# A new hand-out order for the matrix products of an attention-and-MLP kernel, and a later place for one small product

## The chip, the cores and the metric

The kernel runs on one core of a Trainium2 chip. The metric is the device time of one execution, in microseconds (us): the median of three runs. A core has a matrix engine (TensorE, PE in the profile), three engines for elementwise work (VectorE, DVE; ScalarE, ACT; GpSimd, POOL), and SyncE (SP), which here only issues transfers. Products are accumulated in eight PSUM banks; a bank holds 128 partitions by 512 float32 values. All other tiles lie in the on-chip memory SBUF, and DMA queues, which the engines issue to, bring data from and to the chip's DRAM.

## The reference

Two stages: an attention block over four batches of 12,480 tokens of 128 features, then a two-layer perceptron over all 49,920 tokens.

```python
# x[4,12480,128], inducing[32,128]; scale = 1/sqrt(128)
def mab(q, kv):
    a = softmax(scale * (q @ kv.T))
    return a @ kv
h = mab(inducing, x)        # 32 rows of 128 for each batch
y = mab(x, h)               # every token: weights over the 32 rows of h
# w_in[128,2048], w_out[2048,128], alpha[2048]
t = y @ w_in
g = maximum(t, 0) + alpha * minimum(t, 0)
out = g @ w_out             # float32, [49920,128]
```

## The kernel before

**How the work is folded.** A token's `y` is a mix of the 32 rows of `h`, so `y @ w_in` is the token's 32 unnormalised weights times `hW = h @ w_in`. The first layer is thus a product over only 32 rows. The exponentials of the scores are made batch by batch (`e`, written to DRAM as `e2d`, and read back as the tile `rep`, in which the 32 weights of the tokens stand in the 32 partitions of each of the four row tiles). Normalisation is left to the end: the finished output is multiplied by the reciprocal of the sum of weights (`rdT`).

The activation is split in two. Its relu part goes through `W1 = (1 - alpha) * w_out`. The rest is linear in `t`, so it needs no wide layer: `Amat = w_in * diag(alpha) * w_out` (128 by 128) is made once, and `hA = h @ Amat` once per batch. `Amat` takes 16 products of `winT` and `AW` (alpha times `w_out`, made on POOL) that are added up in one bank; this is `w_amat` (lines 952 to 959), called `am` in the tables, and `hA` is made by `h_linear` (line 632), called `hl`.

**Groups, fills and second products.** The tokens are worked on in 100 groups, 25 per batch: 24 of 512 tokens and one of 192. TensorE's 128 rows are used as four row tiles of 32 rows, numbered 0 to 3, on which products of 32 rows can run side by side. A group has 16 *fills* (`fill`, line 733), 4 per row tile: a 32-row product of `hW` and `rep` writes 128 channels by 512 tokens into a bank, and ScalarE (line 750) or VectorE (line 752) evicts the bank with a relu into a bf16 tile `gt`, of which there are 80. (The group of 192 tokens has 8 fills of two products each.) After that come the *second products* (`second`, line 784): each `gt` tile is multiplied with `W1`, again in four parts of 32 rows, and all 64 parts of a group are added up in one bank, the group's *home*. Row tile 0 does its 16 parts of a group, then row tile 1, and so on; on one bank a row tile starts only when the one before it is through (`hand_over`). The product with `hA` is one more product into the same bank. The last three groups (`WHOLE = 3`) use products of all 128 rows instead, 16 for each group. When row 3 has ended a group, `finish` (line 809) transposes the bank on VectorE (line 818), multiplies it with `rdT` on POOL (line 826), and POOL issues the transfer to the output (line 851).

**The order.** Nothing is scheduled by a program: every engine's order is written out by hand. The string `PLAN` is read token by token (the loop at the end of the function), and `pin` holds every engine to the order in which instructions are issued:

- `a` to `h`, with a digit for the bank: a fill. The letter's index divided by two is the row tile; even letters (a, c, e, g) are evicted by ScalarE, odd ones (b, d, f, h) by VectorE.
- `w`, `x`, `y`, `z`: the next second product of row tile 0, 1, 2, 3.
- `l` and `m`, with a digit for the bank: a group gets its home bank. For groups from the third on (`LATE = 2`) the product with `hA` is issued here; for the first two it is issued at the group's end. `v` is a whole product of 128 rows, for the last three groups.
- `s`, with digits for banks: a pause. The functions of the next line of `PAUSES` are called, with those banks to work in, and then those of the line with the same key in `BEHIND`.
- a lone digit 0 to 3: a *useless* product (`useless`, line 761) on that row tile. It multiplies old `xT` data into bank 4 + r, and nobody reads it.

`PAUSES`, `EVENTS` and `BEHIND` are keyed by group and fill. `EVENTS` are run just before the fill with that key. A pause, however, stands where its `s` stands in `PLAN`; its key only sets the order of the pauses. Before the change `am` is issued ahead of fill 32 (counting all fills from 0) and `hl0` ahead of fill 42.

The functions behind the names that matter here: `rep` loads a `rep` tile from `e2d`, four transfers on SP's queue; `new` takes new tiles for a batch; `xa` transposes the first half of a block of `x` for the next batch, by transposing transfers on SP's queue; `den` makes the sums of weights, whose reciprocal comes back as `rdT` over SP's queue.

Of the kernel before, what the change touches and what calls it, by code (L numbers as in the profile page):

```python
# [30 lines left out]
1 8 am  # L31
2 2 hl0
# [35 lines left out]
1 8 rep01  # L68
# [120 lines left out]
1 8 new1 xa10  # L189
# [14 lines left out]
3zwc4wzwf1zxwe6zwh7xwzc3wzxwg4d1wzxwe6xzwf7zwzc3ywywzd4ywzc1yzl6yxwg7yxg3wxywh4xywxya1xywxyh2a7x  # L204
ywxyb3xya4xywd1ywxe2wxzf7s342zf1xwzxwe3zxwf7zwc2zwyc4zwyd1zwyzyc3zyxb7zyxg2yxb4zyxza1yxzyxb3ze7x
zyxl2yxwg4yxwyxwg1yxwh3yxwxg7wf4xzwxe0zwze1wzywd3zywzyc7wzyd4wzyc0wzwf1zwyza3yza7xyzb4xyza0xzyxl
1zyxwyxwg3yxwh7xywg4yxwh0xywg5xwzxe3wxzwf7xzwxze4wxf5zwc0zwzd3yws745d0wzywyzc3b7yzyzxa4yzxl5yzxb
0yzxa3yzxwzxywxg7ywxg4ywyxh0wyg3xwyxwyxh7wxe6wxzf4wxze0wxze3wzwd7zywc6zywzywd4zyc0zyxb3zyxzya7xz
yb6xzya4xzyl0xzywxg3ywxzywxg7ywxyh6wxywg4xe3wxzwxf2zwxzwe7xzwe4d6zwyzwyd3zwyzc2wyzd7wyza6yzl4xyz
wxyg3b2xyzxwyza6xyzb7xyzwxyg3wxyg2wxyh6ywxwxwxe7zs312xzb7e6xzwf3xzwe2xzwzwc1zywd6yzwc7yzwd2yzwza  # L210
3yzyb1xyzxa6zyxl7zyxwh2yxa3yxzwyxwg6yxwg1yxwyxwh3yxwg2xwe6xwzf5xwzxwze1xwzf3c2wzwzywd6yzwc5yzyzd
# [12 lines left out]
yg2wxyg5wxyh4wxwxf1zwxe3zwzwc2yzwyd5wzyc4wzyzl3d1yzwxyza2xyzwxf5zwxe4zwxyzb1xyza2xywzxyzwc5ywxyg
4wxyg1b2xywxywxe5b7xzwe4xzwd2zwxe1zwd5zwyc7zwyzc4yb2zxyl1zxywzxya5h7yxwzyxwg4d2ywzywxza5yxzyb7xz
xywg4ywxzywxg2yxwe5wxf7wzxf4xzws2657wxzf2wzc4wzyd6wzyc7l5zywwzxywwwzxe2b4zxywwzxywa7h6xywwxzywwx
zwe2wb4xyzwxwzya7xzyl6xywxg2ywxyh4wxywg7xywxwf0c2zwyxzxwxyxh4wc7yzxwyxzxwxe2d0zwyxzxwyxzwc7f4zxw
yxzxwyc2zb0yxzxxyza7xyzb4xyzxya2zxyzl0xywg7xywxyh4ywyxe2zwxyzwyxyyh3we7xzwyxyzywyxe4h2wxyzwyxyyz
wyc7f3zwyzwyc4zwyd2zwyzwc7yzyb3zxya4zxyzxa2yzxl7yzxzwyzzxa3zf4zxzwzyzxzwzyg2xywh1xwyzxg3wyxzzwxz
ze4wzxf2wzxwe1zxwzf3c5wzywzyc4wzyd2wzyc1zwyb3zyza5xyzxyb4zxya2zxyl1xzywxze3xwyh5xwyg4xwyxwyg2xwy  # L230
h3s6452xzwf3xzwe6xzwe4xzwf2xzwc5zwzwyd3wzywd6zywc4zya2zyl5zyxwh3yxwzyxwg4yxb6zyxwzyxa2yzxwyxwyg3
xwyxh4ya6xwe2xwxzf0wxzwxe3zwxzf6wzc4wzywd2zywc0zyzya3zxb6yzxyl4zxywzc2b0yzxywzxya3zxywg6xywxyh2w
xywg0xyg3wxywh7xwe6xzwxzwf2xzwe0xzwd3zwyzc7wyzwyza6d2yzl0xyzwxyg3wd7yzwxyzwxe6zb2xyzwxyza3xyzwxy
a7xywh6xyg2wxywxyg3wxf1wxwzxe7wzxf2zwc6zwyzwd3yzc1yzxa7yzxb2yzxl6yzxwyzc3b1yzxwyzxwyg7xb2yzxwyzx
we3zwxyg1wxywxywxh7ys23517xwzf2xwze3xwzf7c5wzwzyc1wzyd2wzya3zyzyxb7zyxa5zyxb1zyxl2zyxwze3xwzyd7w
yxg5wyxzwyxg1wyxg3wyxh7wyxwxg5wxzf1wxze4wxzwzd3wzyc7wzyd5wzyc1l4zyxwzyxa3zf7xwzyxwze1xzb5yxzwyxz
a3yxzwyxg7wyxwh1yxa5yxwg3yxwyxh0wyxwe7xwzf5wc1zywzywd3zywc0zya7zyxb5zyxl1zyxwzyc3b0zyxwzyxwg7f5x
wzyxwzyxa3zf0xwzyxwg7yxwzyxwg5yxwf3xwe0zxwzxwze7wd6zywzywc5yzd0l3zwxe7zwxzyb6xzywc5yzwxyzxb0yzxa
7zyxwyh6xa5yzxwyzxwyg0xwyxwg7yxwyh5xws60275h6we0xwzxwzd2e5zyc7wzywzyd0l6zyxwzyxa5zyd2wzyxwg7yxwz
f0xwzyxa5zyxwh2yxwze7xwzyxwh0yxa5yzxwyxza2yxg7wxwzxf0wze5wzywd2zywc4zya7zyxzb0yxzl5yxzwyxg2b4yxz  # L240
wyxzwyc7h0wyxzwyxza2yxh4wyxzwyc7zwyxzwe0xwf2zxwzxe4wzxwzxe7wzd0wzywzc1yl4zd2ywzxya7zxywh0xywzc1y
wzyxb2zyxa7zyxwzyxa0zyxwg1yxwyxwh2yxwg7yxwxf0we3xzwf1xzwze2xwzwzc7wyzd0yl3zwyxzya2xh1ywxzxya7zxy
b0zxywzc2wyzd1wyzxa7yzwxyzwxyg0wxyh2xwyg1wxye7wxwxzf0s6127f0zxwe6zxwzd1we7zwyzc2yzxyb0zxyzxya6zy
xb7zyxa1zyxl2zyd0wzyxwg6yxwh7yxwzyc1wzyxwg0yxwh6xywxwe7xzwxe1zwxzwf0c5zwyzwd7yzwc6yzwd1yza0yzxl5
yzxwyzxa7f6zxwyzxwyg0xb1yzxwyzxa7yzxwyg6xwyh0xwyxg1wyxwe7xwzxf4wzxe6wzwzyd1wzyc0wzyd7wzya4zya6xz
yxzb1yxzl0yxzwyd7zwe4xzwyxzwe6xzwyxg1wyxwh4yxwyg7xwyxh6wyxa3xe1wzxwzf4xwze7wzywzd3ywzc6yl1zyxwh4
yxwg7yxwzyxb3zyc6wzyxwzyxa4h7yxwzyxwzyd3a6zyxwzyxwg4yxwzxe7wzxwzxb6s34273e6wzd4f7wzxe2wzxs3yc6wz
# [876 lines left out]
```

## Time and profile before

| | us |
|---|---|
| three runs | 541.54, 541.55, 541.62 |
| median | 541.55 |
| the profiled execution: its span | 540.4 |
| TensorE busy | 526.3 (97%) |
| VectorE busy | 504.2 (93%) |
| ScalarE busy | 496.3 (92%) |
| GpSimd busy | 394.7 (73%) |

The profile is of one execution. Its span, from the first to the last thing recorded, is 540.4 us; the runs' times hold about 1.15 us more, which lie outside of the span. "Busy" is the time in which an engine worked on at least one instruction. For TensorE this says little here, since four row tiles can work at once and one is enough to count as busy. Other views used below: the groups of instructions (line, engine, operation, output tile `<-` input tiles, shape, count, then busy time, mean in ns, and idle time ahead of them with what ended it), the chain of waits (start, length, engine, what), the timeline (start, length, engine, line, what), and stretches of the span (start:end, length, then busy time and instruction count of PE, PEld, DVE, ACT, POOL, the granted share of TensorE's clock, the busy share of the DMA engines, and GB/s).

### The profile page before, as it was taken

The numbers are of one execution on the slowest core, as the hardware profiler recorded it, in microseconds if no ns is written. First come the engines' busy times: TensorE is split into PE (matmuls) and PEld (weight loads), VectorE is DVE, ScalarE is ACT, GpSimd is POOL, SyncE is SP. The second block draws the span as 40 slices with busy tenths as digits, with TensorE's granted clock in tenths as the row PEclk, the third lists the DMA queues.
The fourth block names the chain that finished last, engine by engine and source line by source line (L and its number), as shares of the span: only waits on it lengthen the run. The fifth ranks groups of instructions, "written<-read, shape, count | busy, mean of one in ns | idle before, by whom it ended". The sixth has DMA issues, their size and how long they took to land.

```text
span 540.4 us, 21603 instructions
## 1 busy us (share of the span) xinstructions
PE 526.3 (97%) x8988; PEld 332.7 (62%) x8988; DVE 504.2 (93%) x865; ACT 496.3 (92%) x994; POOL 394.7 (73%) x574
## 2 busy tenths in 40 slices
PE   4999999999999999999999999999999999999996
PEld 4655566566567566666667666666666566666653
DVE  3699999999989999999998999999999999999994
ACT  2499999999989999999999999999999999999950
POOL 5553778687667987687687987776767876776764
PEclk9999999999999999999999999999999999999998
DMA  8999999987799898887799797864354344334324
GB/s 197 212 186 139 182 185 156 170 142 113 112 175 149 134 160 152 162 129 145 117 153 166 117 164 158 168 101 113 66 93 113 66 96 112 70 89 108 68 42 85
DMA packets 114738, 71.12 MB, mean 132 GB/s; under 512 B 86784, under 2 KB 102784, under 8 KB 114640
## 3 DMA queue, kind: packets, MB, share of 16 engines
q0 software_dynamic: 19456, 38.62, 38.9%
q1 hardware_dynamic: 91984, 30.22, 32.9%
q8 instruction: 70, 1.15, 0.9%
q10 hardware_dynamic: 3200, 0.90, 0.7%
q14 instruction: 28, 0.23, 0.2%
HBM read 41.00 MB, written 28.95 MB: 129 GB/s over the span
## 4 chain that ended last, share of the span: by engine, by line
PE 90%; DMA 4%; DVE 2%; ACT 1%; POOL 1%; issue 1%; SPq 0%; POOLq 0%; DVEq 0%
PE bank L383 90%; DMA xn<-in_x_dram 2%; DMA rep<-e2d 1%; ACT gt L750 1%; DVE gt L752 1%; DMA e2d<-e 1%; POOL xn L412 0%; DVE ot L818 0%; PE bank L458 0%; ACT e L656 0%; DVE xT L461 0%; POOL ob L826 0%; DVE fr L608 0%; SPq L671 0%; POOL out_dram L851 0%
## 5 line engine op out<-in xcount | busy, mean ns | idle before, releaser
L383 PE MATMUL bank<-gt,W 32*128 32x512 bf16 (+1 forms) x6256 | 480.3, 371 | 0.1
L750 ACT ACTIVATE gt<-bank 128x512 bf16<-128x512 f32 (+1 forms) x906 | 464.5, 612 | 6.9 <-PE bank L383 4.6
L752 DVE TENSOR_SCALAR gt<-bank 128x512 bf16<-128x512 f32 (+1 forms) x662 | 417.7, 677 | 9.9 <-PE bank L383 6.1
L383 PE MATMUL bank<-rep,hW 32*128 32x512 bf16 (+1 forms) x1600 | 418.4, 368 | 1.5 <-DMA rep<-e2d 1.3
L383 PEld LDWEIGHTS <-W 32*128 32x128 bf16 x6256 | 264.4, 92 | 146.5 <-issue 46.6
L851 POOL DMA_DIRECT2D out_dram<-ob x386 | 247.3, 669 | 37.7 <-POOL ob L826 30.4
L826 POOL TENSOR_TENSOR ob<-ot,rdT 128x512 f32<-128x512 f32 (+2 forms) x99 | 106.3, 1074 | 93.8 <-DVE ot L818 79.5
L383 PEld LDWEIGHTS <-hW 32*128 32x128 bf16 x1600 | 136.9, 92 | 20.8 <-issue 5.1
L818 DVE STREAM_TRANSPOSE ot<-bank 128x512 f32<-128x512 f32 (+1 forms) x100 | 69.9, 699 | 6.7 <-PE bank L383 5.6
L383 PE MATMUL bank<-rep,hA 32*128 32x512 bf16 (+1 forms) x100 | 36.1, 367 | 0.0
L427 POOL DMA_DIRECT2D xn<-in_x_dram x32 | 20.7, 663 | 0.1
L481 ACT ACTIVATE e1t<-bank 128x256 bf16<-128x256 f32 (+2 forms) x14 | 5.0, 356 | 10.8 <-PE bank L383 10.8
L461 DVE COPY xT<-bank 128x1024 bf16<-128x1024 bf16 (+1 forms) x13 | 8.5, 650 | 4.9 <-PE bank L458 4.4
L383 PE MATMUL bank<-xT 32*128 32x512 bf16 x81 | 12.5, 376 | 0.0
L553 ACT ACTIVATE e<-bank 128x512 bf16<-128x512 f32 x18 | 11.0, 610 | 0.2 <-PE bank L383 0.2
L656 ACT ACTIVATE e<-bank 128x512 bf16<-128x512 f32 x18 | 11.1, 614 | 0.1
L383 PEld LDWEIGHTS <-xT 128*128 128x128 bf16 (+1 forms) x177 | 8.0, 97 | 4.1 <-issue 1.5
L383 PEld LDWEIGHTS <-hT 128*32 128x32 bf16 (+1 forms) x122 | 3.6, 93 | 11.0 <-issue 10.9
L383 PE MATMUL bank<-xT,hT 128*32 128x512 bf16 (+1 forms) x98 | 10.3, 388 | 0.0
L383 PEld LDWEIGHTS <-hA 32*128 32x128 bf16 x100 | 9.2, 92 | 1.8 <-issue 0.6
L458 PE MATMUL bank<-ident,xn 128*128 128x128 bf16 x96 | 9.0, 249 | 1.0 <-DVE xn L963 0.9
L412 POOL DMA_DIRECT2D xn<-in_x_dram x11 | 6.2, 583 | 3.3 <-DMA xn<-in_x_dram 2.5
(87 smaller groups left out, 131.7 us busy)
## 6 DMA issues: line engine op xcount, KB each, us to landing
out_dram<-ob POOLq DMA_DIRECT2D x373, 64.0 KB, 3.2
rep<-e2d SPq DMA_DIRECT2D x92, 128.0 KB, 3.2
xn<-in_x_dram POOLq DMA_DIRECT2D x37, 256.0 KB, 5.5
e2d<-e SPq DMA_DIRECT2D x24, 128.0 KB, 3.6
xn<-in_x_dram POOLq DMA_DIRECT2D x4, 512.0 KB, 8.2
rdT<-rt SPq DMA_DIRECT2D x96, 8.0 KB, 2.6
early<-in_moe_w_out_dram POOLq DMA_DIRECT2D x4, 256.0 KB, 10.6
xT<-xn SPq DMA_TRANSPOSE x36, 5.2
```

Of the source, the lines that this page charges most:

```text
L383: return pin(nc.tensor.matmul(o, lhsT, rhs, start=start, stop=stop, **kw))
L412: pin(nc.gpsimd.dma_start(out=xn[:, q0:q1, :], in_=src[:, q0:q1, :]))
L427: pin(nc.gpsimd.dma_start(out=st.xn[u][:, part, :], in_=src[:, part, :]))
L458: pin(nc.tensor.transpose(tp[:, k * P : (k + 1) * P], xn[:, q, j * C : (j + 1) * C], ident[:]))
L461: pin(nc.vector.tensor_copy(out=st.xT[:, u, qs[0] : qs[-1] + 1, :].rearrange("c q t -> c (q t)"), in_=tp[:, : len(qs) * GRP],))
L553: pin(nc.scalar.activation(out=e1[:], in_=ps[:], func=EXP, scale=scale, accum_out=st.es[:, u : u + 1]))
L656: pin(nc.scalar.activation(out=e2[:].rearrange("p (t j i) -> p t j i", j=n, i=32), in_=turned(ps[:pp, :w], n), func=EXP, scale=scale_of(st ...
L750: pin(nc.scalar.activation(out=gt[:, :w], in_=ps[:, :w], func=RELU))
L752: pin(nc.vector.tensor_relu(gt[:, :w], ps[:, :w]))
L818: pin(nc.vector.transpose(out=ot[:, :t], in_=acc[:, :t]))
L826: pin(engine.tensor_tensor(out=ob[:, k0 * w : k1 * w].rearrange("p (k m c) -> p k m c", k=k1 - k0, c=32), in0=ot[:, k0 * w : k1 * w].rearr ...
L851: pin(queue.dma_start(out=dst[a], in_=ob[32 * a : 32 * a + 32, :t].rearrange("p (b k) -> p b k", k=32),))
```

## The change

It does four things.

1. `PLAN` is replaced by another table. It holds the same 1568 fills and the same second products, in another order, with other banks and other engines for single fills (905 fills on ScalarE and 663 on VectorE, where there were 906 and 662). How far the second products stand behind the fills is nearly the same in both tables; how the four row tiles alternate is not. In the old table the rows mostly take turns (`wzyx wzyx`); in the new one the same row often has several products one behind another (`zzzz`, `wwx`, `xyyx`).
2. Useless products: 8 instead of 81. In the new table they stand between fills 10 and 25.
3. The pause with `am` gets the key 2 0 in place of 1 8, `hl0` the key 2 10 in place of 2 2, and their `s` tokens move with the new table: `am` is issued ahead of fill 35 instead of 32, `hl0` ahead of fill 43 instead of 42. The other pauses stand ahead of the same fills as before.
4. `new1 xa10`, which followed behind that pause, become events of key 1 8, right behind `rep01`, ahead of fill 24. On SP's queue the order of the transfers stays the same.

No function is changed. The diff, with the tables cut:

```diff
 PAUSES = """
 0 4 pe01
 0 8 bs01 den00
-1 8 am
-2 2 hl0
+2 0 am
+2 10 hl0
 4 8 bs02 as10 den01
...
 EVENTS = """
 0 0 load11
-1 8 rep01
+1 8 rep01 new1 xa10
 2 1 xb10
...
 BEHIND = """
-1 8 new1 xa10
 4 8 xa12
...
 PLAN = """
-b02h12c223a312s4h212b012a323c12313f413s23e01h112l2wg42d33w231w3e03w32d1w31we431w3f31w3e01w32w3d1
-2w3c42w32wd3g02w132w12h1wc4232xa02h3xa523x23b4x23a1x23xl0w23wxxwf3g5xw3e4s1h5xe3wxe4w3xwf13xw23x
-wxe3wh5x2w32wc43wyd13wyc6wg3ys5b4yya1d6ywya5yyg3xb43xy3ya1xyxh6yc53yxh3ya4x3xy3xb1xza6zl5xe7zwxf
...
-zwzyc4zyxzb7yxza1yxzyb2xyzl0xyzwxyza4xyh7xwzyc1wzywxzyxwg2yxwh4ywxyg7wyxs1d5e2zwxzwxzwe7zwxf4zwe
-1zwyc2zwyd5zwyd7zya4zxya1zxyzxyb2zxyg5xyzd4yg7xyzxyh1xya2zxyxyg5xyh4xe7xzxf2zxe1zxzc5e6zyzb7yzyb
-4zc1yzyzyh5yh2yb6zyd7zyzyzyh1ym4zyb5zvvvvvvvvvvvvvvvvyd2m6h7yh1d5vvvvvvvvvvvvvvvvzzd3m4zzzzzf2zz
-zzb7f1b5zzzzzvvvvvvvvvvvvvvvv
+b0g1c2f3h4s5f6l1d0wwa2s35a4e23wwwh63g3wwb03c4w3c5wf2a63wh3wwwc0d4g5w3wwd23l6g3wxwwxg0wxf4x3wxe7f5wxw
+e2a3xxb0xb4wc7wxh5wc2a0s3g4f7b2xxwwe5xxwd0a3wxe4e7xws5c2yywb3yxyl0xwyh4c5xxywxwg7wyh3yxwwh2xxyyg4xyw
+ya5b7e3yxwyxd4wxwg2yyxb5wwxze7xf3zzzxwc4zwyc2ywyzwd5ze7yxzxb4zya3yzyyxd2xxzza5a7yxzzf4xg3xzyxyxza2yx
...
+wxh6yws71e3wxzxzwf2zwxe6wxzf7wzc1c3yzyyzxb2yxl6zxyzxwg7b1xyzywywyzxc3h2yzwzxyywxa7d1zxwxza3zxyxyg2xw
+ywg7wys1wwxzf3xze0zzwxzwe2d1wyyzzzwc7wyd3yzyc0xh1xya2zzzxyxyb7a3xyzyxxyh0a1yzxyg2zxzyxyxyg7e3xxg1xf0
+zxzzxzf2e4zzyzb7yyc0d3yzza1yzh2yzyyc4yyzzyh7b0zzzf3yym1h4yb2vvvvvvvvvvvvvvvvyyd7b0h5h3m4vvvvvvvvvvvv
+vvvvzd2zzzzb1f7zzzzzm0f5zzd3zzzzvvvvvvvvvvvvvvvv
 """
```

More of the change, by code (lines that the diff above doesn't have):

```diff
@@ L206 @@
[L206 to L211, printed above, removed]
@@ L302 @@
[L302 to L303 removed]
+b0g1c2f3h4s5f6l1d0wwa2s35a4e23wwwh63g3wwb03c4w3c5wf2a63wh3wwwc0d4g5w3wwd23l6g3wxwwxg0wxf4x3wxe7f5wxw
+e2a3xxb0xb4wc7wxh5wc2a0s3g4f7b2xxwwe5xxwd0a3wxe4e7xws5c2yywb3yxyl0xwyh4c5xxywxwg7wyh3yxwwh2xxyyg4xyw
+ya5b7e3yxwyxd4wxwg2yyxb5wwxze7xf3zzzxwc4zwyc2ywyzwd5ze7yxzxb4zya3yzyyxd2xxzza5a7yxzzf4xg3xzyxyxza2yx
+yh5s743l1d2ywxwg5xf7wxg3yxwwywwxf4e2zc5wzyyd7yzzzzwf3wwc4zwyc2wzzywwzyd5e7wzd4yza3yxxyyza2yzxb5l7xwx
@@ new lines @@
+ywzxze4a3xxyxxwwyh2g5wywf4xg6yxwg3wxzzzwxf2wwzzwxwzxe5d4e6wzzwf3yywc2yza5d4yyzxb6yxzyyxza3zzl2d4a5ww
+zwzyyxg3xwyg6xxxyxyh5yxwyg4xxxywg3h0wzwxwze6f5zzxe4wxzwwf0s365d4yywzzc0yywzd6wc3zzwyzzzyxb5yzxa4yb0y
+xa6yyxzl3xxywzg5xwxg4yywwxh6wywxg0xh5wyxwe1xxwzwe4xf6zzwwzwxe0yd5ywzyc1zzwd4wzyzc6yxyzb0xxzya5yza1zx
+xzyb4xyl6wyywyyzxg0xxwwzg5yxywh1xg4xwwe0xwzzwxf7xwe5wzzzxf4c1wyzzyzywd0wc7yzywzyzywc5b4l1zxywxxzb0za
+7yywxxxzzya5ywyg4ywwxxh0g7wxxyxywf5g2wxs407xxwh5e2zzwzwf4xxe7zwc0zwwyd5zyzzwywc2yd7l4zyxxyxzzwa0b5xy
@@ new lines @@
+zyyzxwa2b7yyzywxg0wzxxe5yzxywwxxg2xwh7ywwwyg0xwxf5ze3zwzwxzwxf2yc7zzyzwzyywc0d5ya3xzyb2xyxyzl7yzwxd0
+a5yzwzzxxa3yh2xwywwyyxzzwyxg5xyg0xwxf3xwze2wwwzxwzxf5e6zxzzwd0yywc3zyzyzwd2wa5ya6yzxzb0xl3wzyywxyywz
+yxg5d2zzyxa6zxs0526h1xwxwxyg0h5wyxyg6wwwye2xxf1zxwzze0zwwxwwxf5zzxc6d2wyyzwc1zyb0za5zzyxl6xyxzywc2xy
+b1zxzwyya0zywzc5xywyyxwyxg2h1ywxg0wwwxh4wxxywxe5zf2xze1xzwzwzwwxf0c4yzzwyc5d2yzzxxa1zyxzyb0zxa4xyzyb
+2xyxl5yxwyzg1yxwh0zwyc4yxwyyxwxwwzg2xwwwyg1f0xxze4f7xzws2104f7zyzzwd1wzzwc2ywyzwyc0b4ya7yzyzxxzb2xa1
@@ new lines @@
+zxyyyxl0wxyywzg4h7zxzywxa2zxxyg1ywwyxwxwh4e7zzwwwxxze2wxf3zwxe1wzyzd7wc4wzzyd2zzywyc3b1yzzxyzyl7xya4
+wzxyxb2xg3ywzxyywzyxg1wxywxg4wh2wywwxxwxye3xf6e1zzzxzxwf4zzwxzwc2wc3wyc6wzyyb1b4yxzxl2yxzyyxzyzywa3y
+xwza1d6ywzwzywxxg4xwxzyg3xxywh1wywyxg6s4531e6wzf4xwzxzwe5zwf1wxxc3zzwd6yzwc4yyzzl5ywxzxb1wzzwzyc3zyx
+yb4zxa6xywxzxxyya1xh3yyxwyxwg4ya6wxwyh1xwxwyg0f4wxwxe3zwzzwye6d1ywzyzd0yzywl4c3yzwxzxwza6xf1zzywzyyx
+zxa3d0ywywyza6xxh1wywwzxg3wwxxyxyzg0wyxe6wxh1zzxxzwwe3zzzwxf7wyc0l1zyd6zywxwc3yb7zxwxzza0yyxwyzd6zya
```

165 lines of the change are left out of this document (75 added, 90 removed).

## The prediction, made before the changed kernel was run

> **What bounds the kernel now.** First the page's busy shares, then the span cut into five stages.
>
> ```profile
> PE 526.3 (97%) x8988; PEld 332.7 (62%) x8988; DVE 504.2 (93%) x865; ACT 496.3 (92%) x994; POOL 394.7 (73%) x574
> 24.00:36.00 12.00, 11.80 (x159) 5.38 (x160) 10.69 (x18) 11.28 (x21) 9.78 (x11) 1.00 0.98 167
> 52.00:508.00 456.00, 454.45 (x7996) 289.67 (x7993) 442.76 (x750) 450.13 (x902) 349.23 (x489) 1.00 0.74 130
> 508.00:520.20 12.20, 12.19 (x187) 7.41 (x185) 12.13 (x23) 12.08 (x25) 9.21 (x13) 1.00 0.29 53
> 520.20:540.40 20.20, 15.55 (x101) 7.73 (x95) 12.03 (x23) 0.06 (x1) 9.56 (x13) 0.88 0.39 71
> ```
>
> The columns are PE, PEld, DVE, ACT and POOL. In the long middle three engines are busy together: TensorE 454.45 of 456 us, ScalarE 450.13, VectorE 442.76. No one of them is the bound: a fill writes a bank, ScalarE or VectorE empties it, and the next fill of that bank waits for that. Only the first 12 us and the last 20 us show real room (ScalarE is done at 520.2). Then the chain that ended last, and the groups behind it.
>
> ```profile
> 29.06 21.24 PE bank L383 x306
> 146.56 5.67 DMA rep<-e2d
> 152.28 356.04 PE bank L383 x5940
> L750 ACT ACTIVATE gt<-bank 128x512 bf16<-128x512 f32 (+1 forms) x906 | 464.5, 612 | 6.9 <-PE bank L383 4.6
> L752 DVE TENSOR_SCALAR gt<-bank 128x512 bf16<-128x512 f32 (+1 forms) x662 | 417.7, 677 | 9.9 <-PE bank L383 6.1
> 529.96 1.02 PE L383 MATMUL bank<-gt,W 32*128 32x512 bf16 x4
> ```
>
> The chain runs along TensorE nearly without a break; the one visible hole, the load of `rep` at 146.56, hangs on PAUSES and EVENTS lines that both tables share, so it stays. The evicting engines sit idle before an eviction for only 6.9 us (ScalarE) and 9.9 us (VectorE). The last row gives the price of a product: four of one row tile (all of row 3, that token `z`) one behind another, (1.02 - 0.37) / 3 = 0.217 us from start to start, while the single one takes 0.37. I call 0.217 us a slot.
>
> **The useless products.** 73 fewer. They stand between 24.9 and 41.9 us.
>
> ```profile
> L383 PE MATMUL bank<-xT x81: 372/374/385, 24.9 to 41.9; 32*128 32x512 bf16 x81
> 25.76 1.09 ACT L750 ACTIVATE gt<-bank 128x512 bf16<-128x512 f32 x2 [0.48 <-PE bank L383]
> 28.91 7.39 ACT L750 ACTIVATE gt<-bank 128x512 bf16<-128x512 f32 x13
> 36.86 1.08 ACT L750 ACTIVATE gt<-bank 128x512 bf16<-128x512 f32 x2 [0.56 <-PE bank L383]
> 30.61 4.41 DVE L752 TENSOR_SCALAR gt<-bank 128x512 bf16<-128x512 f32 x7 [0.35 <-PE bank L383]
> ```
>
> 73 slots over four rows are 73 x 0.217 / 4 = 4.0 us of row time, but the rows were waiting there: in these 17 us work comes as fast as banks are emptied. What can be won is what the evicting engines lost. Two ScalarE evictions back to back take a step of 1.09 - 0.60 = 0.49; the 13 from 28.91 on took (7.39 - 0.60) / 12 = 0.57, so 12 x 0.08 = 0.9 us, and 0.48 before them: 1.4 us at most, with 0.35 on VectorE. In the new table row 0 gets its first real products four fills earlier (2 before fill 10, 7 before fill 13, against 0 and 1), and 32 stand before fill 31 against 27, so these steps can come back to 0.49. They need `W`, which POOL makes; the next part shows why little of this is kept.
>
> **The pause for the linear part's product (`am`), and what is behind it.**
>
> ```profile
> 30.43 1.73 SPq L671 DMA_DIRECT2D rep<-e2d  x4
> rep<-e2d SPq DMA_DIRECT2D x92, 128.0 KB, 3.2
> 35.38 1.06 PE L383 MATMUL bank<-early 128*128 128x128 bf16 x16
> 36.37 0.39 PE L383 MATMUL bank<-rep,hW 32*128 32x512 bf16 x1
> 36.89 0.37 PE L383 MATMUL bank<-rep,hW 32*128 32x512 bf16 x1
> POOL ob L826 <- DMA rdT<-rt: 13.8, 1, 13.8
> ```
>
> Fill 33 opens group 2 and needs the first `rep` from DRAM: issued from 30.43 to 32.16, with the 3.2 us of the issues row there by 35.4 at the latest (half the size, so I take 35.0). Nothing in the change moves it. Before, `am` lies in that very wait: 35.38 to 36.44, and fills 33 to 36 start at 36.37, 36.38, 36.60 and 36.89 (the two rows are the first and the last). After, `am` is issued at fill 35: fills 33 to 35 can start at 35.0, `am` follows and ends near 36.3, and fill 36 starts there: 36.9 - 36.3 = **0.6 us earlier**. Bounds: 0, when fill 32 is no earlier; 1.1, the whole of `am`. The new tiles and the first transpose of batch 1 (`new1`, `xa10`) go from behind the pause to the event at fill 24. On SP they keep their place, after `rep01` and before the loads of `rdT`, and the transpose still waits for the last product of `am`; POOL, already 13.8 us in wait for that `rdT`, is no worse off, since `am` ends no later. Cost 0, and if `am` were a microsecond late, still 0, for that wait only holds back outputs.
>
> **The order in the middle.** Counted along the two tables, fills and second products stay level: 1985 against 1986 second products before fill 541, 4450 against 4448 before fill 1141, and row by row within one or two; the pauses fall on the same fills. What differs is how the four rows are mixed: a product directly behind one of its own row occurs 97 times before, 1283 times after. Does such a pair hold back the other rows? Look at the start, where the old table has repeats too.
>
> ```profile
> 28.39 0.39 PE L383 MATMUL bank<-xT 32*128 32x512 bf16 x1
> 28.61 0.38 PE L383 MATMUL bank<-xT 32*128 32x512 bf16 x2
> 29.06 0.37 PE L383 MATMUL bank<-gt,W 32*128 32x512 bf16 x1
> 29.07 0.39 PE L383 MATMUL bank<-xT 32*128 32x512 bf16 x1
> 29.27 0.37 PE L383 MATMUL bank<-gt,W 32*128 32x512 bf16 x1
> 29.29 0.38 PE L383 MATMUL bank<-xT 32*128 32x512 bf16 x3
> 29.49 0.37 PE L383 MATMUL bank<-gt,W 32*128 32x512 bf16 x1
> 29.51 0.37 PE L383 MATMUL bank<-xT 32*128 32x512 bf16 x1
> 29.55 0.45 PE L383 MATMUL bank<-rep,hW 32*128 32x512 bf16 x2
> 29.70 0.37 PE L383 MATMUL bank<-gt,W 32*128 32x512 bf16 x1
> ```
>
> The second fill of the row at 29.55 starts at 29.63 (0.45 - 0.37 later). From the pause before it, its token `d1` stands behind 4 `w` and 12 useless digits; at 29.63 only 3 `w` and 8 useless ones had started. So one fill went past 5 earlier products of other rows: rows are served apart, and at least 6 handed-out products can be waiting. I count slots along each table, one slot for a product on its row, handing out in order as long as fewer than k handed-out ones have not started. k = 1: 2260 before, 3037 after; k = 4: 2223 and 2249; k = 5: 2220 both; k = 6: 2218 and 2215. With the 6 that the rows show, the mixing costs nothing (-3 slots). It may help a little: from fill 200 on about one product more is out before each fill, work for the rows while a fill waits for its bank. Bounds: gain, ScalarE's idle 6.9 less the 1.4 + 0.56 of the start and some 1 us of the `rep` hole, 4 us; loss, 26 slots of k = 4, 5.6 us. Nearest to zero, I take **-0.5 us**. One eviction changes engine (905 and 663 against 906 and 662), -0.49 and +0.59 on engines that run side by side: 0.
>
> The Trainium skill speaks against this part: "TensorE: Matmul & The Clock Gate", section "The mechanism" of Part 3, has matmuls start and end strictly in program order. By that rule the count is the one for k = 1 (rival 2); the rows above differ from it.
>
> **The end.** After ScalarE's last fill the old table has 24 products on row 3 and 13 on row 2 besides the 48 whole ones, the new one 21 and 8, and 14 against 15 fills, all VectorE's.
>
> ```profile
> 517.81 6.03 DVE L752 TENSOR_SCALAR gt<-bank 128x512 bf16<-128x512 f32 x10
> 528.76:532.17 3.41, 3.41 (x28) 1.51 (x27) 2.20 (x5) 0.00 (x0) 1.89 (x2) 1.00 0.32 58
> 532.17:535.58 3.41, 3.41 (x19) 2.29 (x17) 2.14 (x5) 0.00 (x0) 0.87 (x1) 0.50 0.69 115
> L383 PE MATMUL bank<-gt,W 128*128 128x192 bf16 x16 | 2.7, 364 | 0.0
> 27.00:30.41 3.41, 3.34 (x52) 1.47 (x49) 3.25 (x6) 3.33 (x7) 3.39 (x5) 1.00 0.76 163
> ```
>
> Three products on the longest row are 3 x 0.217 = 0.65 us, one VectorE fill (6.03 - 0.69) / 9 = 0.59: **-0.6 us**. And the clock: the stretch at 528.76 is busy throughout, yet its 28 products are mostly of one row, a quarter of the array, and the next stretch gets 0.50 of the clock, just under the last 16 whole products (2.7 us). With the end about 1.7 us earlier, more of those fall ahead of the drop; at full clock they would take half, so 0 to -1.3, and I take **-0.5**.
>
> **The sum.** -0.6 - 0.5 - 0.6 - 0.5 = -2.2 us, against the execution profiled: 540.4 to 538.2. The runs' median is 541.55, 1.15 above that span; kept, this gives **539.4 us**.
>
> **The rivals.** 1, *slower: fills queue behind their own row.* A fill directly behind a product of its row: 2% of ScalarE's and 1% of VectorE's before, 17% and 11% after, some 136 + 66 more. On average such a one is half a slot, 0.108 us, late: 14.7 us on ScalarE, 7.1 on VectorE, some 11 us of the whole if all of it reaches the evictions. For it: in the middle those engines have no slack. Against: the row would have been about as busy in the old order, since each row's own sequence is the same. It decides from a fifth on (2.2 us); at 40% the time is 539.4 + 4.4 = 543.8. Chance 0.30.
> 2, *strict order over the rows*: 3037 - 2260 = 777 slots, 169 us, 710 us. The fill at 29.63 speaks against it: 0.02. (This is the skill's rule named above.)
> 3, *the clock falls at the start.* The useless products are about 16 of the 52 in the stretch at 27.00. With 8 left in all, the array is fuller only by the earlier real ones; if a stretch falls under what 528.76 had, 3.41 us run at half clock, 1.7 us lost: 541.1, no change. For it: 28 products were too few. Against: some 45 remain. 0.08.
> 4, *nothing*: fill 32 not earlier, the end eaten by another wait, 540.5 to 542.6, middle 541.5. Changes this far from the bound often end so: 0.12.
> 5, *the middle gives its 4 us*: 539.4 - 3.5 = 535.9. 0.08.
>
> **How the numbers follow.** The forecast itself has 0.40. Its own range is 537.5 to 541, since each term may be 0. What a measurement of this kernel can tell from no change is about 0.2%, 1.1 us. Faster: 0.36 of the forecast, 0.08 of rival 5 and some of rivals 3 and 4: 0.47. Slower: most of rival 1, rival 2 and edges of 3 and 4: 0.34. Same: 0.19. For 8 in 10 the range takes in rival 5 and rival 1 up to a little over half its full price (11 x 0.6): 535.5 to 546.
>
> **What would show it.** Right: the first group-2 fills near 35.0 and `am` behind them; ScalarE's run from 29 us at steps near 0.49; 905 evictions of about 612 ns and ScalarE idle under 6.9 us in all; row 3's fifteen-odd last products starting earlier by 1.5 us. Rival 1: longer idle time before L750 and L752 "<-PE" in 52 to 508, spread evenly. Rival 3: a stretch of 0.50 clock between 27 and 38. Rival 2: fills never ahead of earlier products, TensorE's chain longer everywhere. The forecast is wrong if the middle, from fill 100 to ScalarE's end, changes by more than 2 us either way.

## The result, and the profile after

The changed kernel takes 591.88 us (median of four runs, 591.62 to 592.23), the kernel before 541.59 us beside it. The ratio is 1.0907, with a 95% interval from 1.0876 to 1.0939: 50 us slower. The forecast was 539.4, with a range from 535.5 to 546.

The page of the profile after: busy time of the engines, then the two groups of evictions and the transposes at the end of a group (line numbers are 6 lower than before).

```profile
PE 572.7 (97%) x8914; PEld 332.1 (56%) x8915; DVE 515.6 (87%) x866; ACT 511.6 (87%) x993; POOL 394.4 (67%) x574
L744 ACT ACTIVATE gt<-bank 128x512 bf16<-128x512 f32 (+1 forms) x905 | 479.2, 599 | 41.9 <-PE bank L377 32.4
L746 DVE TENSOR_SCALAR gt<-bank 128x512 bf16<-128x512 f32 (+1 forms) x663 | 425.3, 680 | 40.0 <-PE bank L377 31.8
L812 DVE STREAM_TRANSPOSE ot<-bank 128x512 f32<-128x512 f32 (+1 forms) x100 | 70.0, 700 | 15.0 <-PE bank L377 13.4
```

The rows of ScalarE hold the whole loss: it is idle ahead of evictions for 41.9 us instead of 6.9 (35.0 more), and its evictions are busy for 479.2 us instead of 464.5 (14.7 more, since evictions that come one behind another overlap by some 0.12 us, 0.60 long at steps of 0.48, and single ones do not). Together 49.7 us; the span grew by 590.5 - 540.4 = 50.1. What ended the idle time is TensorE, though TensorE is "busy" for 97% as before.

The stretches of the profile after (columns: PE, PEld, DVE, ACT, POOL with counts, granted clock, DMA share, GB/s):

```profile
52.00:152.00 100.00, 99.30 (x1538) 54.03 (x1536) 89.50 (x152) 91.35 (x181) 67.86 (x96) 1.00 0.85 137
152.00:252.00 100.00, 99.08 (x1630) 60.47 (x1627) 91.12 (x149) 91.84 (x180) 71.78 (x103) 1.00 0.78 138
252.00:352.00 100.00, 99.51 (x1644) 59.92 (x1637) 88.30 (x150) 92.55 (x181) 75.00 (x107) 1.00 0.74 132
352.00:452.00 100.00, 99.08 (x1589) 54.45 (x1587) 89.70 (x152) 91.48 (x176) 64.39 (x90) 1.00 0.52 100
```

All four are alike: some 180 ScalarE instructions in 100 us, where the old kernel had 902 in 456 us, 198 in 100. So the loss is spread evenly and at full clock, and the DMA engines have no more to do than before (a share of 0.85 in the first of these stretches, 0.94 in the old kernel's). It is no single wait that got longer.

Start and end do what was forecast. The timeline: ScalarE's long run at the start, the fills of group 2 and `am`, and ScalarE's last run. Then two stretches of the end, and the group of the last whole products.

```profile
28.10 8.23 ACT L744 ACTIVATE gt<-bank 128x512 bf16<-128x512 f32 x16
34.75 0.38 PE L377 MATMUL bank<-rep,hW 32*128 32x512 bf16 x1 [0.38 <-DMA rep<-e2d]
34.76 0.60 PE L377 MATMUL bank<-rep,hW 32*128 32x512 bf16 x2
35.29 1.07 PE L377 MATMUL bank<-early 128*128 128x128 bf16 x16
36.29 0.39 PE L377 MATMUL bank<-rep,hW 32*128 32x512 bf16 x3
...
567.82 3.11 ACT L744 ACTIVATE gt<-bank 128x512 bf16<-128x512 f32 x6
```

```profile
578.80:582.21 3.41, 3.41 (x28) 1.39 (x26) 2.78 (x6) 0.00 (x0) 1.08 (x1) 1.00 0.44 77
582.21:585.62 3.41, 3.41 (x19) 2.34 (x17) 1.53 (x3) 0.00 (x0) 0.87 (x1) 0.53 0.44 77
```

```profile
L377 PE MATMUL bank<-gt,W 128*128 128x192 bf16 x16 | 2.7, 366 | 0.0
```

The first fills of group 2 start at 34.75 instead of 36.37, `am` lies behind them, and ScalarE's long run has steps of (8.23 - 0.60) / 15 = 0.51 us instead of 0.57. Counting fills from 0 in both traces, fill 34 comes 1.62 us earlier, fill 35 0.60, fill 44 1.22, fill 60 0.44; at fill 100 the new kernel is behind, and from there it loses 3.5 us with every 100 fills.

Where does it wait? The records around 238 us, put beside the program's order, show one such wait; here they stand as the program hands them out (not a view of the profile; start and end in us):

```
row  what                                   start    end
 2   second product                         237.795  238.169
 2   second product                         238.011  238.385
 2   second product                         238.221  238.595
 0   second product, last of row 0's group  237.587  237.966
 1   fill 605                               237.813  238.184
 0   product with hA                        237.824  238.203
 1   first product of that group on row 1   238.663  239.047   hand-over
 3   second product                         238.667  239.051
```

And the same moment in the timeline, VectorE's row, and in the view of waits (who waited, for whom: us in total, times, longest):

```profile
238.68 0.69 DVE L746 TENSOR_SCALAR gt<-bank 128x512 bf16<-128x512 f32 x1 [0.31 <-PE bank L377]
```

```profile
PEld L377 <- PE bank L377: 0.6, 1, 0.6
DVE gt L746 <- PE bank L377: 0.3, 1, 0.3
```

Row 0's last product had ended at 237.966, and row 1 waits for nothing else; yet its first product starts at 238.663, 0.07 us after the third product of row 2 has ended. Fill 605 was in its bank at 238.184, and VectorE, idle, begins with it at 238.68. Both wait as if nothing were done before the three products of row 2, which were handed out earlier, are done. The trace also records every step of the semaphore by which TensorE signals ends: there is none between 237.780 and 238.618, and then two, at 238.618 and 238.652, for these two products. (The ends in the table are those of the profile's records, which it models.)

That is **theory A (signals in order)**: rows start apart, but a product counts as done, for whoever waits for it, only when all products handed out before it are done. The rivals: **B**, a short queue (about two products can wait; counted along the tables, 2438 slots in place of 2177, 57 us); **C**, rival 1 of the prediction, a fill directly behind a product of its own row; **E**, hand-overs placed too close behind one another (87 nearer than 6 products, 16 before); and, for the start, **F/G** further down. The counts in the expectations go along a table: 0.216 us for a product on its row, evictions at their steps, banks, hand-overs and, for A, the signal in order. They are estimates, no measurements.

### The profile page after: what moved, and what is told of

Same layout as the page of the kernel before. It is cut to its first block, busy times and chain, and to the rows that moved or that the text cites. A ratio compares the mean times of both kernels' runs of the same rounds, so it can differ in the third digit from the quotient of the medians.

```text
span 590.5 us, 21453 instructions
## 1 busy us (share of the span) xinstructions
PE 572.7 (97%) x8914; PEld 332.1 (56%) x8915; DVE 515.6 (87%) x866; ACT 511.6 (87%) x993; POOL 394.4 (67%) x574
## 4 chain that ended last, share of the span: by engine, by line
PE 91%; DMA 3%; ACT 2%; DVE 1%; POOL 1%; issue 1%; SPq 0%; POOLq 0%; DVEq 0%; ACTq 0%
PE bank L377 91%; DMA xn<-in_x_dram 2%; ACT gt L744 2%; DMA e2d<-e 1%; DMA rep<-e2d 1%; DVE ot L812 0%; POOL xn L406 0%; DVE gt L746 0%; PE bank L452 0%; SPq L665 0%; DVE xT L455 0%; POOL ob L820 0%; POOL out_dram L845 0%; DVE fr L602 0%; POOLq L1113 0%
## 5 line engine op out<-in xcount | busy, mean ns | idle before, releaser
L377 PE MATMUL bank<-gt,W 32*128 32x512 bf16 (+1 forms) x6255 | 526.2, 372 | 2.1 <-issue 0.2
L744 ACT ACTIVATE gt<-bank 128x512 bf16<-128x512 f32 (+1 forms) x905 | 479.2, 599 | 41.9 <-PE bank L377 32.4
L746 DVE TENSOR_SCALAR gt<-bank 128x512 bf16<-128x512 f32 (+1 forms) x663 | 425.3, 680 | 40.0 <-PE bank L377 31.8
L377 PE MATMUL bank<-rep,hW 32*128 32x512 bf16 (+1 forms) x1600 | 430.8, 369 | 2.0 <-ACT gt L744 0.9
L377 PEld LDWEIGHTS <-W 32*128 32x128 bf16 x6256 | 271.0, 92 | 193.3 <-PE bank L377 45.8
L377 PEld LDWEIGHTS <-hW 32*128 32x128 bf16 x1600 | 131.0, 92 | 25.1 <-issue 7.5
L377 PE MATMUL bank<-xn,e1T 128*32 128x128 bf16 x288 | 7.4, 220 | 0.3 <-DVE ot L812 0.2
L452 PEld LDWEIGHTS <-xn 128*128 128x128 bf16 x96 | 6.8, 112 | 1.5 <-DVE xn L957 1.0
```

The source lines that it names most:

```text
L377: return pin(nc.tensor.matmul(o, lhsT, rhs, start=start, stop=stop, **kw))
L452: pin(nc.tensor.transpose(tp[:, k * P : (k + 1) * P], xn[:, q, j * C : (j + 1) * C], ident[:]))
L744: pin(nc.scalar.activation(out=gt[:, :w], in_=ps[:, :w], func=RELU))
L746: pin(nc.vector.tensor_relu(gt[:, :w], ps[:, :w]))
```

## The experiments

**Tests of rows and signals by themselves (e1).** The edit in short, at seven pauses (`ahead(n, r, bank)` hands out n products on row r, `one` and `test` a single one, and `reads` has ScalarE read the banks; `ahead` stands on line 1048, the product that is read or waited for on line 1052, the single one of the hand-over tests on lines 1064 and 1069, the read on line 1032):

```diff
+ahead(n, 1, a); test(2, b); reads((b, a))           # n = 8, 4, 16, 32
+test(2, b); ahead(8, 1, a); reads((b, a))
+ahead(8, 3, c); i = one(1, a); hand_over(i); test(2, a)
+i = one(1, a); ahead(8, 3, c); hand_over(i); test(2, a)
```

> The kernel before, with seven short tests added at pauses; nothing is left out. In each, all rows are idle first; then products of 512 columns are handed out on named rows, and ScalarE reads the bank of the last one. Tests 1 to 4: 4, 8, 16 or 32 products on row 1, then one on row 2, whose bank is read. Test 5: first the one on row 2, then 8 on row 1. Test 6: 8 products on row 3, one on row 1, then one on row 2 that waits for the one on row 1 (a hand-over). Test 7: the same, but the one on row 1 ahead of the 8. Theory A (signals in order): rows start apart, but a product counts as done only when all handed out before it are done. Then the read comes about 4 x 0.217 + 0.2 = 1.1 us after the first product's start with 4 ahead, 1.9 with 8, 3.6 with 16, though row 2 starts at once with 4 ahead; with it first (test 5) within 0.5 us; in test 6 row 2 starts about 1.9 us after the first product, in test 7 0.45 us. Rival B (a short queue, about two products waiting): with 8 ahead row 2 starts only after 6 slots, 1.3 us, and is read 0.4 us later; tests 5 and 7 as A, test 6 1.75 us. Rival C (only a fill's own row holds it back): row 2 starts at once and is read 0.4 us later in all tests; in test 6 at 0.45 us. Tests 3 and 4 also show how many products can be handed out and not started: with n of them row 2 starts when (16 - n) or (32 - n) slots are over.

The timeline of the test with 8 ahead, of the one with the 8 behind, of the two hand-over tests, and of the one with 16 ahead:

```profile
52.42 1.23 PE L1048 MATMUL bank<-W 32*128 32x512 bf16 x5 [0.37 <-ACT pt L1032]
53.28 0.38 PE L1052 MATMUL bank<-W 32*128 32x512 bf16 x1
53.92 0.37 PE L1048 MATMUL bank<-W 32*128 32x512 bf16 x1
54.40 0.34 ACT L1032 ACTIVATE pt<-bank 128x64 bf16<-128x64 f32 x2 [2.04 <-PE bank L385]
...
70.18 0.37 PE L1052 MATMUL bank<-W 32*128 32x512 bf16 x1
70.59 0.22 ACT L1032 ACTIVATE pt<-bank 128x64 bf16<-128x64 f32 x1 [0.18 <-PE bank L1052]
...
127.63 1.24 PE L1048 MATMUL bank<-W 32*128 32x512 bf16 x5
128.50 0.38 PE L1064 MATMUL bank<-W 32*128 32x512 bf16 x1
128.71 0.81 PE L1048 MATMUL bank<-W 32*128 32x512 bf16 x3
129.61 0.38 PE L1052 MATMUL bank<-W 32*128 32x512 bf16 x1
...
147.85 0.37 PE L1069 MATMUL bank<-W 32*128 32x512 bf16 x1 [0.37 <-ACT pt L1032]
147.86 1.25 PE L1048 MATMUL bank<-W 32*128 32x512 bf16 x5
148.74 0.38 PE L1052 MATMUL bank<-W 32*128 32x512 bf16 x1
...
106.63 2.96 PE L1048 MATMUL bank<-W 32*128 32x512 bf16 x13 [0.37 <-ACT pt L1032]
109.23 0.39 PE L1052 MATMUL bank<-W 32*128 32x512 bf16 x1
```

With 8 ahead, row 2's product is over at 53.66, but it is read at 54.40, 0.11 us after the last of row 1 has ended (53.92 + 0.37). With the 8 behind it, it is read 0.04 us after its own end. That the reader waited for more than one signal is no way out: with 8 ahead, row 2's product is the only one of the nine that steps TensorE's semaphore, and the step comes at 54.32. In the first hand-over test row 1's product is over at 128.88, and row 2 starts at 129.61, 0.09 us after row 3's last has ended (129.52). A holds, B and C do not. There is a limit too, though not B's: row 2 starts when the fifth of 8, or the 13th of 16, starts on row 1, and with 4 ahead with the first; so three products of one row can be handed out and not started, and the next one holds back everything. That is why the second hand-over test gave 0.89 us, not the 0.45 of A: it stood behind the fifth of the eight as well.

**The same products in another order (e2 to e6).** A stretch of the tables, from fill 615 on, shows the edits:

```diff
-a2yxg7wxwzxf0wze5wzywd2zywc4zya7zyxzb0yxzl5yxzwyxg2     old table
+a2xyg7zxxwwf0wze5yzwwd2wzyc4yza7zzyxb0xyzl5wzyyxxg2     before_adj
-a0wwzwyxg4zzwxf1e7zywc0wyzd3zzya4yxb1yxzzl7yxzwyxa0     new table
+a0xwwxwzg4xxwzf1e7zzyc0wwyd3yzza4yxb1zyxzl7xzywxya0     after_lag
+a0zywxwwg4xwzzf1e7wzyc0wzyd3zyza4xyb1zxyzl7xyzwxya0     after_rot
+a0wwzwyxg4wxzzf1e7zywc0wyzd3zzya4yxb1yxzzl7yxzwyxa0     after_hand
+a0zyxwwxg4xzzwf1e7wwzc0zzyd3yzya4zxb1yxzyl7yzxxwya0     after_deal
```

> The old table; between two fills its second products are sorted so that those of one row follow one another (2382 products directly behind one of their own row, 97 in the old table, 1283 in the new). What is handed out between two fills is unchanged. A (signals in order): counted along the table, with evictions at steps of 0.49 and 0.60 us and signals in order, 14 us more than the old table, where the same count gives 38 of the 50 us for the new one: 555 to 562 us. B (two products waiting): 2532 slots against 2177, 355 x 0.217 = 77 us: about 618. C (fills directly behind their own row: 143, against 22 before and 234 after): 121 / 212 x 50 = 29 us: about 570.

> The new table with its fills, engines, banks, homes and pauses where they are; only which row has which of the places of second products is dealt anew, so that, counted along the table, fills are held back least by slower rows ahead of them. As many products as in the new table stand directly behind their own row (1270, 1283 there). A (signals in order): the count falls by 32 of 38 us: 545 to 555 us. B (two products waiting): 2402 slots against 2438, -8 us: about 584. C (209 fills behind their own row against 234): -6 us: about 586.

> The new table; between two fills its second products are put into turns as far as that goes (463 directly behind their own row instead of 1283), but each stretch between two fills keeps the products it had, so that a row with many in one stretch still falls behind. A (signals in order): the count falls by 10 of 38 us: 575 to 582 us. B (two products waiting): 2272 slots against 2438, -36 us: about 556. C (143 fills behind their own row against 234): -21 us: about 571.

> The new table with 136 second products exchanged with one close by, so that the first product of a row in a group stands at least 6 products behind the last one of the row before it (7 hand-overs stand nearer than 6, 87 in the new table, 16 in the old); nothing else is moved, and rows are mixed as unevenly as before (1338 products directly behind their own row). Rival E (hand-overs placed too close): rows are idle ahead of a row's first product for 57.4 us (mean over the four rows) in the new profile against 26.1 in the old; that comes back, 31 us: about 561. A (signals in order): what a hand-over waits for is the slowest row handed out before it, so a few places more help little; the count along the table falls by 1.7 of 43 us: 586 to 592 us.

> As the run after_lag, dealt again with a count that also has what the tests showed: at most three products of a row that are handed out and not started, 36 ns from the last end to an eviction, 61 ns more at a hand-over, all rows empty at a pause. Fills, engines, banks, homes, pauses and the order of the groups' ends are those of the new table; 1255 products stand directly behind their own row (1283 in the new table), 208 fills (234). A (signals in order): the count falls by 31 of 43 us, and the new table lost 50 where the count gives 43: 591.9 - 36 = 556, between 550 and 565. C (own row): 26 fills of 212 fewer, -6 us: 586. E (hand-overs too close: 55 nearer than 6, against 87): 32 / 71 x 31 = 14 us: 578.

Measured, with one run each, while the kernel before took 540.8 to 546.4 us on the same chip: before_adj 567.4, after_lag 571.2, after_rot 578.2, after_hand 590.8, after_deal 564.7 us. In after_lag three fills (208, 864 and 1056) write into the home bank of a group whose second products are not all done, so its output is wrong and its time may hold waits that the others lack; the argument stands without it. B is out: it wanted 618 for the first and 556 for the third. E is out: 80 hand-overs moved apart brought about 1 us, no more than such runs differ by, where 31 were asked. A got after_rot, after_hand and (just) after_deal, and was 5 us low for before_adj and 16 for after_lag. C got before_adj within 3 us, and was 7 to 21 us off in the others. So A explains the most, and something beside it grows with products of one row standing together.

What that is can be read from the traces. For each eviction that found its engine idle, the records tell whether the fill was already in its bank (and held back by an earlier product on another row), or had itself started late, and behind what. Sums over ScalarE and VectorE between 60 and 500 us, worked out from the records with the program's order beside them (before_start and best are told of below):

| idle ahead of evictions, us | before | after | before_adj | before_start | best |
|---|---|---|---|---|---|
| all | 13.1 | 63.3 | 32.5 | 11.0 | 22.0 |
| fill done, held back by an earlier product | 1.4 | 40.1 | 10.6 | 1.2 | 3.3 |
| fill late, its own row busy | 4.6 | 12.1 | 12.0 | 4.8 | 13.2 |
| fill late, behind a hand-over | 0.3 | 4.0 | 2.1 | 0.3 | 1.5 |
| other (its bank, another fill, not told) | 6.8 | 7.3 | 7.6 | 4.7 | 4.0 |

The groups of the profile have 13.7, 72.0, 35.9, 11.6 and 23.6 us of idle time in the same stretch, so the table does not hold all of it. Of the 50.2 us that it grew by (a sum over two engines, and so not the 50 us of the run), 38.7 are held-back signals, 7.5 are C, 3.7 hand-overs. Half of all evictions begin at least 0.27 us after their fill's own end in the new kernel, 0.12 in the old one; against the end of all earlier products it is 0.13 and 0.10, and hardly one begins less than 0.036 us after that.

**Only the start of the change, in the old table (e7, e9, e10).**

```diff
-...g5xw3e4s1h5xe3wxe4w3xwf13xw23x...       old table
+...g5xwe4h5xe3wxe4wxws7f1xwxwx...          before_start: 8 useless products, am at fill 35
+...g5xwe4s1h5xe3wxe4wxwf1xwxwx...          before_few: 8 useless products
+...g5xw3e4h5xe3wxe4w3xws7f13xw23x...       before_am: am at fill 35
```

> The old table with only the start of the change: 8 useless products (the first 8) instead of 81, the pause for am ahead of fill 35 in bank 7 instead of fill 32 in bank 1, new1 and xa10 as events at fill 24. All other tokens as they were. Prediction's terms (am 0.6 us, at most 1.4 us from steps of ScalarE at the start): 1.0 to 1.6 us faster, 540.0 to 540.6. Rival (these things are hidden: work behind them starts no earlier): 541.5. Rival (useless products are needed, the clock falls at the start): 542 to 543.5.

> The old table with the first 8 of its 81 useless products; nothing else is changed. In the run before_start the granted clock was 0.50 from 32 to 44 us and fill 44 came 6.1 us later. Theory F (too few products for the clock): the same here without am having moved: a stretch at 0.50 between 31 and 45 us, fill 44 at 44 to 46 us, 545 to 548 us. Rival G (am's new place or its bank 7 brought the clock down, or made the wait): the clock stays at 1.00 and the time at 540 to 541.6.

> The old table with all 81 useless products; only am's pause is moved ahead of fill 35 (bank 7), with new1 and xa10 as events at fill 24. F: the clock stays at 1.00; fills 33 to 35 start about 1.3 us earlier, since they no longer stand behind am, and fill 36 at most 0.6 us: 540.9 to 541.6. G: fill 36 comes 4 us or more later, at 0.50 of the clock: 545 or more.

Measured: before_start 547.8 (ratio 1.0119, 1.0091 to 1.0147), before_few 545.7 (one run, while the kernel before took 540.3 to 545.6, so here the trace tells more than the time), before_am 542.6 beside 542.3 (1.0007, 0.9993 to 1.0020). Stretches of before_few, then two of the changed kernel:

```profile
27.00:30.41 3.41, 3.21 (x28) 1.43 (x29) 3.41 (x8) 3.40 (x7) 3.39 (x5) 1.00 0.74 154
30.41:33.82 3.41, 3.35 (x20) 1.19 (x18) 2.57 (x4) 2.35 (x5) 3.41 (x5) 0.56 0.96 220
33.82:37.23 3.41, 3.41 (x21) 1.01 (x16) 1.58 (x3) 2.00 (x5) 0.39 (x1) 0.50 0.95 157
37.23:40.64 3.41, 3.41 (x31) 2.27 (x32) 1.48 (x3) 1.73 (x4) 0.00 (x0) 0.50 1.06 222
```

```profile
27.00:30.41 3.41, 3.41 (x36) 1.86 (x37) 3.41 (x8) 3.41 (x8) 3.39 (x5) 1.00 0.84 158
30.41:33.82 3.41, 3.38 (x38) 1.42 (x36) 3.06 (x6) 3.40 (x8) 3.41 (x5) 1.00 0.94 221
```

F is right: without the useless products the old table has 28 products in a stretch, 8 of them a pause's, and 20 in the next, and the clock falls to 0.56 and then 0.50 for some 10 us, which costs 3.7 us at fill 44 (6.1 with `am` moved as well, whose 16 products then take 1.89 us instead of 1.07). The new table keeps the clock with 8 useless products, because it has 36 and 38 products there. Rival 3 of the prediction was a real danger, and what averted it is the earlier second products of row 0. It was averted narrowly: after_deal has the same 8 useless products and the same fills, only its second products in another order, and its clock fell behind a stretch with 25 products:

```profile
31.82:35.23 3.41, 2.44 (x25) 0.74 (x20) 2.58 (x4) 2.82 (x6) 2.44 (x4) 1.00 1.03 203
35.23:38.64 3.41, 3.41 (x29) 2.21 (x31) 1.72 (x4) 1.68 (x3) 0.00 (x0) 0.50 0.98 174
```

At fill 40 after_deal is 0.4 us behind the old kernel, where the changed one is 1.3 us ahead. Moving `am` alone, the clock stays up, fills 33 and 34 come 0.4 and 0.2 us earlier, but fill 36 comes 1.1 us later, and nothing is won.

**The new start with the old order, and a table dealt anew by the count (e8, e11, e12).**

```diff
 new table to fill 63, then the old one, banks renamed          (splice)
-...e7xf3zzzxwc4zwyc2ywyzwd5ze7yxzxb4zyze3z...                  splice
+...e7zf3wzxxzc4wzyc2wzwzyd5ye7zzyxb4zyze3z...                  splice_deal
-a2yxg7wxwzxf0wze5wzywd2zywc4zya7zyxzb0yxzl5yxzwyxg2            old table
+a2xzywxg7xwzf0wxwze5wzyd2wzc4yyza7zxyzb0zxyl5xzywyxg2          best (with the start of before_start)
```

> The run before_start, with second products and fills dealt anew within some ten places along the whole table, so that counted along it fills are held back by slower rows for 7 us in all instead of 37 (the old table's profile shows 28.9 us between 52 and 500 us). 925 products stand directly behind their own row. A (signals in order): the count falls by 1.6 us under before_start: 538 to 540. C (own row: 138 fills against 22): 116 / 212 x 50 = 27 us slower, about 567. A, with what the count lacks (it gave 19 of 26 us for before_adj and 17 of 30 for after_lag): up to 545.

> The new table up to fill 64 (the first of group 4), then the old one, with its banks renamed so that the homes agree; a few second products at the seam are left to the earlier or later half so that each row has all of its own. So: the start of the change with the old mixing of rows. In the new kernel's profile fill 34 came 1.62 us earlier and fill 60 still 0.44. A (signals in order; from there on the order is the old one): that is kept, 540.6 to 541.4. Rival H (something else of the new table, not its order from group 4 on, costs the 50 us): 585 to 592.

> The run splice, with the second products between fills 43 and 76 dealt anew among their places so that no row falls behind. A: of the 1.62 us that the new kernel had ahead at fill 34 some 0.6 more is kept than in splice: 540.0 to 541.0. If the re-dealt stretch goes as the re-dealt tables before_adj, after_lag and best did, slower than counted: 541 to 542.

Measured: splice 541.8 (1.0004, 0.9983 to 1.0025), splice_deal 542.1 (1.0002, 0.9984 to 1.0019), best 562.0 (1.0380, 1.0345 to 1.0415). The splice settles the place: with the old table from fill 64 on, the 50 us are gone, and ScalarE is as it was. With the order the splice also takes back the old banks, engines and pauses there, so it does not tell these apart; after_deal, which changes the order alone, brought back 27 of the 50 us, and the table's row of banks and other fills grew by only 0.5 us. ScalarE in the splice's profile:

```profile
L744 ACT ACTIVATE gt<-bank 128x512 bf16<-128x512 f32 (+1 forms) x906 | 464.6, 609 | 5.8 <-PE bank L377 3.1
```

But the gain of the start does not last either: fill 34 comes 1.45 us earlier than in the old kernel's profile, fill 60 0.28, fill 100 0.03 later. Between fills 40 and 64 it is still the new order that runs, and it gives away what the start won; splice_deal, dealt anew there, is ahead by 0.1 at fill 60. The run best fell: before_start's own order lost nothing after the start, best loses some 15 us more than it from fill 60 on, though hardly a fill is held back by another row (3.3 us in the table). Its profile:

```profile
L744 ACT ACTIVATE gt<-bank 128x512 bf16<-128x512 f32 (+1 forms) x906 | 467.2, 608 | 17.4 <-PE bank L377 13.3
L746 DVE TENSOR_SCALAR gt<-bank 128x512 bf16<-128x512 f32 (+1 forms) x662 | 417.6, 678 | 17.6 <-PE bank L377 13.3
```

There C is the largest part (13.2 us of 22.0 in the table, 4.8 in before_start). The count had placed every fill behind its own row at a moment when that row should just have come free; that on the chip it had not is the likely reason, but no run tests it. No version was found that beats the old kernel.

## Why the prediction was wrong

**The step that failed** is the order in the middle: "With the 6 that the rows show, the mixing costs nothing (-3 slots)", taken as -0.5 us. It measured +50: from fill 100 to the end the new kernel falls 49 us behind, and with the old table from fill 64 on (splice) the loss is gone. The rows at 28.4 to 29.7 us were read rightly: a fill did start ahead of 5 earlier products, and e1 shows the same. But a start is not what the next engine waits for. The count had no place for the signal of a product's end, and this goes out in order. In the old table the rows mostly take turns, so that no row is far behind the others; in the new one three products of a row stand together, and a fill behind them is done, like fill 605, 0.41 us before anyone may know. The bound of 5.6 us on the loss came from the same count, and so was no bound. What the runs leave open is how the 50 us divide: 38.7 of the 50.2 us of idle time in the table are held-back signals, and no new deal of the rows alone brought back more than 27 us of the run.

The prediction had set the rows against the rule of the Trainium skill ("TensorE: Matmul & The Clock Gate", section "The mechanism" of Part 3), which has products start and end strictly in program order, and took the rule as refuted. Half of it was: starts are not in order (row 2 at 53.28, ahead of three of row 1). For ends the rule's use holds: the same section calls one signal on the last product sound because of it, and the read at 54.40 and the start at 129.61 agree, though the recorded ends themselves, 53.66 and 54.29, are not in order.

**Rival 1** named the right sign and the right place to look ("longer idle time before L750 and L752 '<-PE' in 52 to 508, spread evenly"), but for a mechanism that makes 7.5 of the 50 us of idle time. Its argument against itself, that each row's own sequence is the same, is true of that part and says nothing about what waits across rows. **Rival 2**, strict order, would have cost 169 us; the chip lies between.

**Useless products and `am`**: right, but not kept. The prediction counts fills from 1 in this part, so its fills 33 to 36 are 32 to 35 here. The first three start at 34.75 (35.0 forecast), `am` ends at 36.36 (36.3 forecast), and fill 35 starts at 36.29 in place of 36.89: 0.60 us earlier, where 0.6 was taken. ScalarE's steps fell from 0.57 to 0.51, where 0.49 was hoped for. Alone in the old table neither edit wins anything (e9, e10); that the early second products make both possible is shown for the useless products by the clock, and only likely for `am`. Left alone, the gain is used up by fill 80 (splice), so its place in the sum should have been near 0. **The end**: from the end of ScalarE's last fill (570.93, 520.26 before) it takes 19.5 us instead of 20.1: 0.6, as forecast, though no run tests the reason. The 0.5 for the clock did not come: the 16 last whole products take 2.7 us as before, and the stretch after 28 products gets 0.53.

**Moved `new1 xa10`, the changed bank and engine digits**: nothing of them shows; the splice, which has the former, is level with the old kernel. Banks and engines were not changed alone in any run. **The pauses** do not all stand ahead of the same fills in the two tables, as was said ahead of the prediction and in it: the one with key 4 8 stands ahead of fill 72 instead of 80, the one with key 7 0 ahead of 118 instead of 120, and six others differ by one fill. Only three of these eight lie between fills 120 and 1500, where the loss grows evenly, so they are not what costs the 50 us.

## What to carry to other kernels

When products of several row tiles run side by side, count their ends in program order: whoever waits for one product waits for all that were handed out before it, on any row. So hand the rows out in turns, and put no run of one row ahead of a product that another engine waits for; where a count along the program says that starts are free, ask the same of the signals. And a useless product may be what keeps the clock up: before removing it, count the products in each stretch of some 3.4 us without it.

Counting helped to explain, not to design: the count gave 43 of the 50 us for the change, but the table it liked best lost 15 us on the chip.

## What the runs showed of the hardware

- Ends are signalled in program order, starts are not: a product that started ahead of three of the eight handed out before it on another row was over at 53.66, but the semaphore stepped at 54.32 and it was read at 54.40, when the eight were over at 54.29.
- Three products of one row tile can be handed out and not started; with 8, 16 and 32 ahead the next row started with the fifth, the 13th and the 29th.
- TensorE 94% busy (3.21 of 3.41 us) with 28 products, most of them of 32 rows, was followed by a clock of 0.56 and 0.50 (before_few), and 72% busy with 25 by 0.50 (after_deal); with 36 and 38 it stayed at 1.00 (the changed kernel).
